# Fetches of row lists declared free of the stores of later groups, in a fused convolution and mixture-of-experts kernel

## The chip, the cores and the metric

The kernel runs on one core of a Trainium2 chip. The metric is the device time of one execution in microseconds (us); less is better. The core has five engines that run side by side, each through its own list of instructions in order: TensorE (PE in the profile, with its weight loads as PEld), VectorE (DVE), ScalarE (ACT), GpSimd (POOL) and SyncE (SP). An instruction that has to wait for a semaphore holds up everything behind it on its engine. Transfers are issued by SyncE and GpSimd and run on 16 shared DMA engines.

## The reference

Inputs: `x` of 8 x 3584 x 192 values, weights for 7 taps of 8 heads per token, and 8 experts of a 192 to 1024 to 192 network. First a causal convolution whose taps are a softmax of each token's own weights, then each token goes to the one expert whose embedding has the largest cosine with it.

```python
w = exp(weight_gen - max(weight_gen)); w = w / (sum(w) + 1e-9)     # over the 7 taps
out[b, s, h] = sum over k of w[b, s, h, k] * x_pad[b, s + k, h]    # causal, 24 values a head
logits = normalized(out) @ normalized(expert_emb).T / tau
expert_idx = argmax(logits); gate_w = softmax(logits)[expert_idx]
result[token] = gate_w * (relu(out[token] @ w1[expert_idx]) @ w2[expert_idx])
```

## The kernel before

The 28672 tokens are worked on in 32 units of 128 x 7 tokens. VectorE multiplies and adds the taps of a unit; for the first five units TensorE does the additions (`sums=5`), in PSUM. ScalarE squares, scales and splits the rows into two 16-bit parts, SyncE turns them with a transposing DMA (`turn`, L519), TensorE computes the logits, VectorE chooses the expert and counts each token's place in its expert's list. GpSimd then writes each token's row into the list of its expert in `lst`, a tensor in device memory, with indirect stores of 128 rows, seven for a unit (`scatter`, L625). A unit's rows stand in one of three buffers, `row_0x` to `row_2x`, in turn.

Units go in 18 groups: the first four of one unit, then 14 of two. After most groups a batch of eight tiles is made, one for each expert, of 256 rows (`T`) or 128 rows (`P`); which, is written in `sizes`. VectorE computes in `schedule` from where in each list the tile is read: only lists with enough rows take part, others read rows that go nowhere. So a tile reads rows that were stored by the time of the batch, while later stores go to places above them in the same list. At the end come 28 tiles of 128 rows for what is left in the lists (`last_batch`), behind `pads` (L1559), which writes empty rows behind each list's end.

A tile begins with `fetch` (L684), called by `load_rows` (L674) on SyncE: it reads the row number into a register, issues a transposing DMA of the rows into `x_0x`, `x_1x` or `x_2x` and a small DMA of the gates and token numbers into one of six `meta` buffers. From the ninth tile on three `x` buffers are used in turn, so a fetch must also wait until TensorE has read the tile three before. For a large tile ScalarE copies a part (`again`), then TensorE does the first layer (`first`, into PSUM banks `bank_..`), ScalarE the relu (`hi`), VectorE the low part (`lo`), TensorE the second layer (into `gram` and `bank_02x`), ScalarE scales it, GpSimd stores it (`out_dram`).

The order on every engine is written out ahead by a planner (`run_steps`): a list of steps with estimated costs and priorities is simulated while the program is built, and each step is issued when its turn comes. `InOrder` (L56) keeps each engine to that order; `behind` (L72) puts instructions that are made elsewhere behind the last one. On SyncE fetches, turns and loads of `x` and of the tap weights stand in one order.

Which instruction waits for which follows from what they read and write. A fetch reads `lst` at a place that is known only when it runs, and a `scatter` writes it at such places, so each fetch depends on every store that was issued ahead of it in the order, also those of later groups. Exceptions are declared: a `scatter` is free of other stores (group `rows`) and of fetches (group `loads`); a fetch joins the group `loads` only. `load_rows` also adds by hand the stores of the groups that are new in its batch, `deps`.

Of the kernel before, what the change touches and what calls it, by code (L numbers as in the profile page):

```python
# [24 lines left out]
    groups=(1, 1, 1, 1, 2, 2, 2, 2, 2, 2, 2, 2, 2, 2, 2, 2, 2, 2),  # L25
# [55 lines left out]
def tile_dynconv_moe(  # L81
# [78 lines left out]
    def raw_ins(i):  # L160
        return getattr(i, "ins", i)
# [51 lines left out]
    rows = [a[:, 0 : U * ROWP].rearrange("p (t r) -> p t r", r=ROWP) for a in packs]  # L213
# [444 lines left out]
    class Tile:  # L658
# [15 lines left out]
        def load_rows(self, row0, deps):  # L674
            def fetch():
                return self.fetch(nc.sync.value_load(row0, min_val=0, max_val=DUMMY))

            for i in SP.behind(fetch):
                i = raw_ins(i)
                tc.add_to_no_dep_group("loads", i)  # L680
                for d in deps:
                    tc.add_manual_dep(i, d.name, sync_dep, reason="rows of the lists")

# [446 lines left out]
    groups, group_of = [], {}  # L1130
# [611 lines left out]
```

## Time and profile before

| what | value |
|---|---|
| median of 3 runs | 1236.18 us (1232.36 to 1238.47) |
| profiled execution | 1239.12 us, of it 1237.3 us from the first to the last instruction |
| mean granted TensorE clock | 0.974 |
| TensorE busy | 1138.2 us (92%), 13376 matmuls |
| TensorE weight loads busy | 997.3 us (81%) |
| VectorE busy | 1018.2 us (82%) |
| ScalarE busy | 802.7 us (65%) |
| GpSimd busy | 616.7 us (50%) |
| DMA moved | 156.15 MB |

Busy time is time in which an engine executes; waiting and issuing of transfers are not in it. SyncE only waits and issues, so it has no busy time, and its timeline shows its transfers. Shares are means over stages that differ: up to about 200 us the first units and the weights are prepared, to about 980 us units and tiles run side by side, then only tiles are left. A wait is put down to what ended it.

### The profile page before, as it was taken

Reading aid. Unit: us, or ns where it says so; the run is one execution under the profiler, and the core shown is the slowest. Engines: PE = TensorE matmul, PEld = TensorE weight load, DVE = VectorE, ACT = ScalarE, POOL = GpSimd, SP = SyncE. Lnnn points to the kernel's source line nnn. Section 1 sums busy time; section 2 is a strip of 40 time slices with the busy share of each in tenths; the row PEclk is TensorE's granted clock in tenths of the full one; section 3 lists DMA queues with packets and bytes.
Section 4 is the critical chain, followed back from the end, with each engine's and each line's share of the span. In section 5 each row is a group of like instructions: output and inputs, shape, how many; then the busy total and the mean of one; then the engine's idle time right before and its main releaser. Section 6 shows DMA issues by size and latency. Waiting matters only on the chain. (4 is left out here: it accounts for less than half of the span.)

```text
span 1237.3 us, 34717 instructions
## 1 busy us (share of the span) xinstructions
PE 1138.2 (92%) x13376; PEld 997.3 (81%) x13376; DVE 1018.2 (82%) x1546; ACT 802.7 (65%) x2036; POOL 616.7 (50%) x566
## 2 busy tenths in 40 slices
PE   5996478989989999989999899999899999999996
PEld 3553267878888898879888788889899989899996
DVE  8997698999988999889899999799797426338884
ACT  1765457779878987979797676566566434444442
POOL 4025143728566584847556576655537352223332
PEclk9998689999999999999999999999999999999999
DMA  9979446566666655755576646554434442112221
GB/s 273 259 188 155 102 124 128 146 139 152 175 138 147 138 141 133 168 129 165 158 140 149 151 126 131 142 103 110 128 61 107 108 118 56 42 44 51 49 43 30
DMA packets 254495, 156.15 MB, mean 126 GB/s; under 512 B 225005, under 2 KB 238565, under 8 KB 251248
## 3 DMA queue, kind: packets, MB, share of 16 engines
q1 hardware_dynamic: 228656, 94.86, 36.3%
q0 software_dynamic: 25664, 58.98, 15.8%
q8 instruction: 106, 1.74, 0.6%
q14 instruction: 69, 0.57, 0.2%
HBM read 62.20 MB, written 46.45 MB: 88 GB/s over the span
## 5 line engine op out<-in xcount | busy, mean ns | idle before, releaser
L66 PEld LDWEIGHTS <-wall 128*128 128x128 f16 (+2 forms) x5316 | 392.7, 99 | 110.7 <-issue 72.7
L66 DVE TENSOR_TENSOR prod_0x<-x_t,w_t 128x1344 f32<-128x1344 f32 x90 | 139.1, 1546 | 0.7 <-PE sums_0x L66 0.7
L66 DVE TENSOR_TENSOR prod_1x<-x_t,w_t 128x1344 f32<-128x1344 f32 x89 | 137.8, 1549 | 0.0
L66 POOL DMA_INDIRECT lst<-row_1x,pos x77 | 101.6, 1320 | 34.3 <-issue 22.2
L66 POOL DMA_INDIRECT lst<-row_0x,pos x77 | 100.7, 1308 | 29.7 <-issue 23.8
L66 POOL DMA_INDIRECT lst<-row_2x,pos x70 | 92.8, 1326 | 41.8 <-issue 21.7
L66 ACT ACTIVATE hi_2x<-bank_00x 128x512 f16<-128x512 f32 x91 | 54.3, 596 | 48.8 <-PE bank_00x L66 28.2
L66 ACT ACTIVATE hi_3x<-bank_10x 128x512 f16<-128x512 f32 x88 | 52.5, 597 | 42.4 <-PE bank_10x L66 22.5
L66 ACT ACTIVATE hi_0x<-bank_01x 128x512 f16<-128x512 f32 x91 | 54.3, 597 | 37.2 <-PE bank_01x L66 25.5
L66 ACT ACTIVATE hi_4x<-bank_11x 128x512 f16<-128x512 f32 x88 | 52.5, 596 | 39.3 <-PE bank_11x L66 24.6
L66 ACT ACTIVATE hi_1x<-bank_12x 128x512 f16<-128x512 f32 x88 | 52.3, 594 | 38.5 <-PE bank_12x L66 26.2
L66 PEld LDWEIGHTS <-hi_1x 128*128 128x128 f16 x744 | 67.6, 99 | 4.6 <-issue 1.8
L66 PEld LDWEIGHTS <-hi_0x 128*128 128x128 f16 x752 | 67.5, 98 | 4.4 <-issue 1.3
L66 PEld LDWEIGHTS <-hi_2x 128*128 128x128 f16 x744 | 66.9, 98 | 3.6 <-issue 0.9
L66 PEld LDWEIGHTS <-hi_3x 128*128 128x128 f16 x704 | 62.8, 98 | 5.4 <-issue 2.6
L66 PEld LDWEIGHTS <-hi_4x 128*128 128x128 f16 x704 | 63.1, 98 | 3.0 <-issue 0.8
L66 DVE TENSOR_TENSOR acc_1x<-acc_1x,prod_1x 128x1344 f32<-128x1344 f32 x42 | 65.0, 1548 | 0.4
L66 DVE TENSOR_TENSOR acc_1x<-acc_1x,prod_0x 128x1344 f32<-128x1344 f32 x42 | 65.0, 1547 | 0.0
L66 PE MATMUL gram<-wall,lo_0x 128*128 128x192 f16 x256 | 63.6, 248 | 0.0
L66 PE MATMUL gram<-wall,lo_1x 128*128 128x192 f16 x256 | 63.0, 246 | 0.0
L66 DVE TENSOR_TENSOR acc_0x<-acc_0x,prod_1x 128x1344 f32<-128x1344 f32 x39 | 60.4, 1549 | 0.3
L66 DVE TENSOR_TENSOR acc_0x<-acc_0x,prod_0x 128x1344 f32<-128x1344 f32 x39 | 60.5, 1550 | 0.0
(434 smaller groups left out, 3614.1 us busy)
## 6 DMA issues: line engine op xcount, KB each, us to landing
x_t<-in_x_dram SPq DMA_DIRECT2D x24, 1248.0 KB
w_t<-in_weight_gen_dram SPq DMA_DIRECT2D x16, 392.0 KB
x_t<-in_x_dram SPq DMA_DIRECT2D x8, 672.0 KB
wall<-in_moe_w_dram POOLq DMA_DIRECT2D x7, 768.0 KB
x_t<-in_x_dram SPq DMA_DIRECT2D x8, 504.0 KB
wall<-in_moe_w_dram POOLq DMA_DIRECT2D x7, 512.0 KB
wall<-in_moe_w_dram POOLq DMA_DIRECT2D x14, 256.0 KB
lst<-pad SPq DMA_DIRECT2D x8, 194.0 KB
```

Of the source, the lines that this page charges most:

```text
L66: self.last = self.tc.keep_in_program_order(op(*args, **kwargs))
```

## The change

One line in `load_rows`. Both transfers of a fetch are declared free of all stores in the group `rows`, with the exception of the stores in `deps`: those of the groups that are new in this batch, and for the last tiles also the pads. Stores of groups that older batches took in had been waited for by the first fetch of those batches, earlier in SyncE's order. The loop at the end for lists that are longer than foreseen calls `fetch` directly and is as before.

```diff
             for i in SP.behind(fetch):
                 i = raw_ins(i)
                 tc.add_to_no_dep_group("loads", i)
+                tc.declare_no_dep(i, group="rows", keep=deps, reason="rows of later groups lie above those that are read")
                 for d in deps:
                     tc.add_manual_dep(i, d.name, sync_dep, reason="rows of the lists")
```

## Rows read from the trace of the kernel before

**Rows 1.** Busy time by stretch: stretch, us, busy us (instructions), clock, DMA share, GB/s.

```profile
200.00:960.00 760.00, 724.33 (x8831) 649.76 (x8829) 686.11 (x909) 579.46 (x1529) 457.33 (x389) 0.99 0.57 136
960.00:1180.00 220.00, 218.65 (x2726) 205.33 (x2724) 122.59 (x249) 96.11 (x212) 73.95 (x70) 1.00 0.28 66
```

**Rows 2.** Waits of SyncE, 200 to 965 us: who, for whom, us, times, longest.

```profile
SPq L66 <- DMA lst<-row_1x,pos: 94.2, 24, 8.9
SPq L66 <- DMA lst<-row_2x,pos: 81.5, 22, 9.5
SPq L66 <- DMA lst<-row_0x,pos: 70.0, 18, 8.8
...
SPq L66 <- DVE row_2x L66: 19.0, 6, 6.0
```

**Rows 3.** Timeline of SyncE: start, us to issue, what it issues.

```profile
471.41 0.42 SPq L66 DMA_DIRECT2D x_t<-in_x_dram  x1
...
583.65 0.36 SPq L66 DMA_DIRECT2D x_t<-in_x_dram  x1
584.83 1.27 SPq L66 DMA_TRANSPOSE x_0x<-lst  x1
...
848.31 1.30 SPq L66 DMA_TRANSPOSE x_0x<-lst  x1
...
871.36 0.36 SPq L66 DMA_DIRECT2D x_t<-in_x_dram  x1
```

**Rows 4.** The chain that ended last: start, us, what; a DMA from issue to landing.

```profile
788.76 4.67 DMA lst<-row_0x,pos
...
872.20 8.41 DMA lst<-row_0x,pos
880.67 2.93 DMA x_0x<-lst
```

**Rows 5.** Timeline of GpSimd: the stores of rows around 757 to 778 us.

```profile
756.01 1.69 POOL L66 DMA_INDIRECT lst<-row_2x,pos  x1 [0.30 <-issue]
...
778.18 1.64 POOL L66 DMA_INDIRECT lst<-row_0x,pos  x1 [1.86 <-issue]
```

**Rows 6.** Timeline of TensorE: matmuls after a gap, in brackets gap and releaser.

```profile
222.94 1.28 PE L66 MATMUL bank_11x<-x_2x,wall 128*128 128x128 f16 x20 [1.80 <-DMA x_2x<-lst]
...
257.59 1.11 PE L66 MATMUL bank_11x<-x_1x,wall 128*128 128x256 f16 x8 [2.68 <-DMA x_1x<-lst]
...
368.44 1.87 PE L66 MATMUL bank_12x<-x_1x,wall 128*128 128x128 f16 x16 [2.98 <-DMA x_1x<-lst]
...
483.04 1.73 PE L66 MATMUL bank_00x<-x_1x,wall 128*128 128x128 f16 x20 [2.76 <-DMA x_1x<-lst]
...
591.47 1.28 PE L66 MATMUL bank_12x<-x_0x,wall 128*128 128x128 f16 x20 [2.86 <-DMA x_0x<-lst]
...
767.09 1.28 PE L66 MATMUL bank_00x<-x_1x,wall 128*128 128x128 f16 x20 [1.71 <-DMA x_1x<-lst]
...
796.61 1.03 PE L66 MATMUL bank_10x<-x_1x,wall 128*128 128x256 f16 x8 [2.20 <-DMA x_1x<-lst]
...
883.65 1.65 PE L66 MATMUL bank_00x<-x_0x,wall 128*128 128x128 f16 x14 [5.43 <-DMA x_0x<-lst]
```

**Rows 7.** Waits of TensorE, 200 to 965 us, of those ended by ScalarE the largest.

```profile
PE bank_00x L66 <- ACT hi_2x L66: 5.0, 2, 3.0
```

**Rows 8.** Waits of ScalarE for fetches, 200 to 965 us.

```profile
ACT x_2x L66 <- DMA x_2x<-lst: 10.1, 5, 3.3
ACT x_1x L66 <- DMA x_1x<-lst: 8.0, 5, 2.7
ACT x_0x L66 <- DMA x_0x<-lst: 5.5, 4, 3.6
```

**Rows 9.** Stretches of low granted clock, first and last of six after 200 us.

```profile
224.28:227.69 3.41, 3.41 (x40) 2.74 (x37) 3.41 (x3) 1.51 (x4) 2.66 (x3) 0.50 0.74 187
...
883.05:886.46 3.41, 2.81 (x25) 2.76 (x25) 0.00 (x0) 0.48 (x1) 0.20 (x1) 0.50 0.32 64
```

## The prediction

> **What bounds the kernel now.** I read the stretches first, then the waits of SyncE, the chain that ended last, TensorE's own timeline and the waits of ScalarE. From 200 to 960 us TensorE is busy for 724.33 of 760.00 us, so 35.7 are lost there; from 960 to 1180 us it is busy for 218.65 of 220.00, which is full [rows 1]. VectorE in the first stretch is busy for 686.11, which leaves it 73.9 us of idle time. So what can be won lies ahead of 960 us, and it reaches the end one for one only where nothing but TensorE sets the pace.
>
> SyncE's queue shows what the edit is about. From 200 to 965 us it sat 64 times (24, 22 and 18), 245.7 us together and 3.8 on average, until an indirect store of rows into the lists (`scatter`) had landed [rows 2]. Some of these waits are needed: the first tile of a batch must wait for the rows of its own groups. But the batch whose first fetch is issued at 848.31 [rows 3] has another one at 880.67, and that one ended a wait for a store issued at 872.20 [rows 4]. A store issued after the first fetch of a batch can't be one that the batch needs, since the first fetch had waited for all of those; it brings rows of the next groups. The other such step of the chain is the store of 788.76, for which the first fetch of a batch waited, at 793.49. This store too is of a later run: the run of stores before it had ended with the one at 756.01, and the next began at 778.18 [rows 5]. The two stores took 4.67 and 8.41 us to land, and the second is followed by 2.93 us for the fetch [rows 4]; from 797 us on the chain is nearly all TensorE.
>
> In TensorE's timeline the reader is to see that its larger gaps end with a fetch: eight of them, 1.80, 2.68, 2.98, 2.76, 2.86, 1.71, 2.20 and 5.43 us, together 22.4 of the 35.7 [rows 6]. Two more, 5.0 us, end with a ScalarE result [rows 7]. ScalarE itself waits 14 times, 23.6 us, for fetches, at the copy that `again` makes of each large tile [rows 8].
>
> **The change, part by part.** It adds no computing instruction and no transfer. For both transfers of each of the 156 fetches it takes away the wait for stores into the lists that are not in `deps`; those in `deps` stay. The order on every engine is written out beforehand by the planner, whose costs the edit doesn't touch, so no instruction moves past another. In a fixed order, a wait taken away can make a later event late only through something shared: the DMA engines or the clock. A few waits that the dropped ones had covered may now be written out (for the store of results that frees a `meta` buffer). I cost them at nothing: they fall into the time in which SyncE idles anyway. Without that cover, at no more than the 0.36 us that the issue of a whole load takes [rows 3], 156 of them would be 56 us of a queue that idled for 245.7.
>
> Now the gaps, one class at a time.
>
> *Fetch held by a store, no load just ahead that is still under way* (gaps at 222.94, 767.09 and 796.61): 1.80 + 1.71 + 2.20 = 5.7 us. The mean hold of 3.8 us is larger than any of the three, so I take all of it; bounds 0 and 5.7.
>
> *Fetch held by a store, with a load of x just ahead of it on SyncE* (483.04 and 883.65). Here one wait hides another. The fetch issued at 584.83, right behind a load of x issued at 583.65, had its matmul begin only at 591.47 [rows 3, 6]: 6.6 us after its issue, against 2.93 on the chain. Counted from the load it is 7.82 us. So the fetch behind the load of 871.36 would be there at 879.2 at the earliest, and if it comes in with the store that travelled beside the same load, at 872.20 + 8.41 = 880.6. TensorE was free at 883.65 - 5.43 = 878.22. The gap shrinks by 3.0 to 4.5 us; I take 3.0, by the store of that very moment. Behind the load of 471.41 the fetch would come at 479.2, before TensorE is free at 480.3, so I take 2.7 of the 2.76. Together 5.7; bounds 0 and 8.2.
>
> The Trainium skill speaks to this: "DMA: Bandwidth & Descriptors", section "Queues, rings and completion order", says that a DMA engine takes the descriptors of one queue in ring order. By it a fetch freed from its semaphore still comes in behind the load, and the 6.6 us above agree; if it did not hold, the gap at 883.65 would close wholly and the sum below be 2.4 us larger.
>
> *Fetch behind a load that itself stands behind a held fetch* (368.44 and 591.47): 2.98 + 2.86 = 5.8 us. These close only as far as the earlier fetch moves up. The mean hold of 3.8 is often enough for that, not always; I take three quarters, 4.4; bounds 0 and 5.8.
>
> *First fetch of a batch, waiting for its own rows* (257.59, 2.68 us): stays. I take nothing.
>
> *Through ScalarE*: 5.0 us [rows 7], the same wait one step on: `again` is late, the relu behind it on ScalarE is late, and TensorE waits for its result. I take three quarters, 3.8; bounds 0 and 5.0.
>
> *The clock.* After 200 us the granted clock fell six times to the lower level (0.50, 1.2 GHz) for 3.41 us; the first and the last are shown [rows 9]. Each begins within 3.5 us after TensorE had fallen idle in one of the gaps above or while it still was. Half of 3.41 is 1.7 us of lost work. I take it away where the gap closes: three of the six (behind 222.94, 483.04 and 796.61), 5.1 us. At 257.59 the gap stays, and at 368.44 and 883.65 a part does. Bounds 0 and 10.2.
>
> What TensorE gets back: 5.7 + 5.7 + 4.4 + 3.8 + 5.1 = 24.7 us.
>
> How much of it reaches the end? After 760 us come the gaps at 767.09, 796.61 and 883.65 and one stretch of low clock: 1.7 + 2.2 + 3.0 + 1.7 = 8.6. From there the chain is TensorE's but for the steps that the edit removes [rows 4], and I carry it whole. The 16.1 us before that lie in shared work: VectorE is busy for 90% of the stretch [rows 1], and ahead of 788 us the chain runs through GpSimd. Carried whole it is 16.1, not at all 0; I take half, 8.0, because TensorE at 95% is the busier of the two, though not by much. Together 16.6 us.
>
> The profiled execution took 1239.12 us: 1239.1 - 16.6 = 1222.5. The median of the runs is 2.9 us below that execution, which gives 1219.6, in round numbers 1220.
>
> **The rivals.** *Another wait takes its place.* SyncE also waits for VectorE before it turns the rows of a unit, 19.0 us in six waits for one of the three row buffers alone [rows 2], and whatever fetch stands behind such a turn stays as late as it was. Against it: just ahead of the fetches for the gaps on the chain stands no such turn. If it holds, only the part after 760 us is left, or less: 0 to 8.6 us, 1228 to 1236. Chance 0.27.
>
> *More than the sum.* The stores of rows stand on GpSimd behind stores of results, which wait for ScalarE, which waits for TensorE, which waits for fetches, which wait for the stores. With that loop cut, the smaller gaps that I didn't count may close as well. The limit is all 35.7 us of TensorE's idle time [rows 1] and 10.2 of low clock: 1236 - 46 = 1190. A likelier point is 30 us, 1206. Chance 0.08.
>
> *Slower.* SyncE comes sooner to the loads of x, which then run ahead of stores of rows; the store beside a load took 8.41 us to land and the other one 4.67 [rows 4], 3.7 more. If that hits the last stores of a group, the first fetch of the batch, which does need them, comes 3.7 us later. Some 15 batches come after 200 us. The 16.6 us and another 6.2 are gone when more than six of them are hit so that TensorE waits; eight cost 30 us, 13 more than the gain: 1249. Against it: of the gaps that I count only the one at 257.59 is of this kind. Chance 0.06.
>
> *No effect.* A wait for a semaphore's count is a wait for all that was counted before; if the stores kept by `deps` share their semaphores with later ones, the fetches could wait as long as now. Against it: the stores in question are issued later than the kept ones, so that their counts are higher. 1236. Chance 0.04.
>
> **How the numbers follow.** The forecast, 10 to 27 us less, has the remaining 0.55; its own range is 1209 to 1226. The limit of 0.5% is 6.2 us, about what a measurement of this kernel can tell from no change. Faster by more: 0.55 + 0.08 and a third of the first rival, 0.72. Within it: the rest of that rival and no effect, 0.22. Slower: 0.06. The range leaves out the deeper half of the second rival, the slower case, and the upper end of the first and the fourth: 1207 to 1235.
>
> **What would show it.** SyncE's waits for stores into the lists should fall from 245.7 to under 90 us. The gaps that now stand at 767.09 and 796.61 should be gone, that at 883.65 should be 2 to 3 us and stand behind a load of x, and the one at 257.59 should stay. ScalarE's 23.6 us for fetches should halve, TensorE's idle time from 200 to 960 us fall to some 15 us, and the low clock to three stretches. The forecast is wrong if these waits go and TensorE's idle time stays, ended by other names: then VectorE or the turns set the pace. It is also wrong if first fetches of batches become late behind loads of x.

## The result and the profile after

The changed kernel takes 1202.53 us (1200.74 to 1206.22, four runs) against 1237.33 for the kernel before in the same comparison: a ratio of 0.9727, 95% interval 0.9688 to 0.9766, 34.8 us less. The direction was forecast, the size was not: 1202.5 lies 17.5 us below the predicted 1220 and 4.5 us below the range.

Busy time by stretch in the profile after (columns as in [rows 1]), with the one stretch of low clock that is left after 200 us:

```profile
200.00:960.00 760.00, 747.63 (x9209) 674.88 (x9209) 698.82 (x945) 592.55 (x1551) 474.68 (x404) 1.00 0.60 141
960.00:1180.00 220.00, 220.00 (x2886) 209.86 (x2884) 138.03 (x267) 96.37 (x213) 71.90 (x65) 1.00 0.23 52
250.60:257.40 6.80, 5.18 (x28) 3.14 (x28) 3.92 (x8) 2.86 (x6) 3.34 (x3) 0.50 0.65 132
```

TensorE's idle time from 200 to 960 us falls from 35.7 to 12.4 us. Of six stretches of low clock, 3.41 us each [rows 9], one of 6.80 is left.

SyncE's waits from 200 to 965 us (who, for whom, us, times, longest):

```profile
SPq L66 <- PE bank_00x L66: 52.4, 21, 8.1
...
SPq L66 <- DVE row_0x L66: 33.5, 7, 7.8
...
SPq L66 <- DMA lst<-row_2x,pos: 9.0, 2, 8.4
SPq L66 <- DMA lst<-row_1x,pos: 7.6, 5, 4.4
SPq L66 <- DMA lst<-row_0x,pos: 6.5, 5, 3.0
```

The 245.7 us that SyncE spent on stores into the lists [rows 2] are 23.1. What it waits for now is room: its waits for TensorE, which must have read an x buffer before it is filled again (the `bank` rows and a few like them), come to 237.3 us where they were 74.9. The fetches now run ahead of TensorE. All waits of TensorE and those of ScalarE for fetches in the same stretch:

```profile
PE bank_11x L66 <- DMA x_1x<-lst: 6.7, 1, 6.7
PE bank_01x L66 <- DMA x_0x<-lst: 2.0, 1, 2.0
PE bank_00x L66 <- ACT hi_2x L66: 1.9, 1, 1.9
PE bank_01x L66 <- ACT lo_1x L66: 0.7, 1, 0.7
PE bank_11x L66 <- DMA x_2x<-lst: 0.6, 1, 0.6
PE bank_01x L66 <- ACT hi_0x L66: 0.5, 1, 0.5
PE bank_11x L66 <- ACT x_2x L66: 0.5, 1, 0.5
```
```profile
ACT x_1x L66 <- DMA x_1x<-lst: 3.0, 1, 3.0
ACT x_0x L66 <- DMA x_0x<-lst: 1.9, 2, 1.3
ACT x_2x L66 <- DMA x_2x<-lst: 0.6, 1, 0.6
```

Seven waits are left where [rows 6] alone show eight large ones, and ScalarE's 23.6 us for fetches [rows 8] are 5.5.

The order of the instructions on TensorE and SyncE is the same before and after, so each matmul and each transfer has its counterpart. The matmuls of 883.65, which waited for 5.43 us, now begin at 845.87 without a gap. Their fetch, issued at 880.67 before, goes out at 836.32, still right behind the load of x that before left at 871.36:

```profile
835.16 0.37 SPq L66 DMA_DIRECT2D x_t<-in_x_dram  x1
836.32 1.58 SPq L66 DMA_TRANSPOSE x_0x<-lst  x1
```
```profile
845.87 1.28 PE L66 MATMUL bank_00x<-x_0x,wall 128*128 128x128 f16 x20
```

The largest gap that remains is at the first fetch of a batch (6.70 us, at 252.22), which needs its own rows; it is longer than its counterpart of 2.68 at 257.59. The last store of those rows left 6.7 us earlier than before (239.80 for 246.46), but took 9.19 us to land, where before the fetch could go out 5.8 us behind it (252.28). The load of x beside it, which left 2.0 us behind that store before (248.42), now left 1.4 us ahead of it:

```profile
238.38 0.53 SPq L66 DMA_DIRECT2D x_t<-in_x_dram  x1
```
```profile
239.80 9.19 DMA lst<-row_2x,pos
249.20 2.97 DMA x_1x<-lst
```

The second gap, 1.97 us at 861.63, stands where before there was none (898.61). SyncE's timeline just ahead of it, and the chain that ended last:

```profile
846.07 1.23 SPq L66 DMA_TRANSPOSE x_2x<-lst  x1
852.79 0.36 SPq L66 DMA_DIRECT2D meta_5x<-lst  x1
853.26 3.41 SPq L66 DMA_TRANSPOSE xT<-row_2x  x1
858.03 2.04 SPq L66 DMA_TRANSPOSE x_0x<-lst  x1
```
```profile
858.03 3.56 DMA x_0x<-lst
861.59 0.04 issue
861.63 1.27 PE bank_01x L66 x20
```

The small transfer into `meta_5x` left 6.7 us after the rows that it belongs to; the longest wait of SyncE between 836 and 862 us is the 5.3 us of the next row, for a store of results out of the same buffer. Behind it comes a turn of a unit's rows (3.41 us to issue), and then the fetch.

```profile
SPq L66 <- DMA out_dram<-o_3x,meta_5x: 5.3, 1, 5.3
```

### The profile page after: what moved, and what is told of

The parts are those of the page before. It is cut to its first block, busy times and chain, and to the rows that moved or that the text cites. A ratio compares the mean times of both kernels' runs of the same rounds, so it can differ in the third digit from the quotient of the medians.

```text
span 1198.8 us, 34709 instructions
## 1 busy us (share of the span) xinstructions
PE 1124.5 (94%) x13376; PEld 990.3 (83%) x13376; DVE 1017.1 (85%) x1546; ACT 803.7 (67%) x2036; POOL 620.2 (52%) x566
## 3 DMA queue, kind: packets, MB, share of 16 engines
q0 software_dynamic: 25664, 58.98, 17.5%
## 4 chain that ended last, share of the span: by engine, by line
PE 78%; DMA 9%; issue 3%; ACT 3%; POOL 3%; DVE 3%; SPq 1%; POOLq 0%; DVEq 0%; ACTq 0%
PE bank_02x L66 18%; PE gram L66 17%; PE bank_12x L66 8%; PE bank_11x L66 8%; PE bank_01x L66 8%; PE bank_00x L66 8%; PE bank_10x L66 8%; DMA wall<-in_moe_w_dram 3%; DMA xT<-row_2x 2%; POOL lst L66 2%; PE g_ps L66 1%; DMA x_0x<-lst 1%; DMA lst<-row_2x,pos 1%; DVE wall L66 1%; SPq L66 1%
## 5 line engine op out<-in xcount | busy, mean ns | idle before, releaser
L66 DVE TENSOR_TENSOR prod_0x<-x_t,w_t 128x1344 f32<-128x1344 f32 x90 | 139.1, 1545 | 0.7 <-PE sums_0x L66 0.7
L66 POOL DMA_INDIRECT lst<-row_0x,pos x77 | 103.3, 1341 | 30.1 <-issue 22.9
L66 POOL DMA_INDIRECT lst<-row_2x,pos x70 | 93.8, 1340 | 43.0 <-issue 22.7
L66 ACT ACTIVATE hi_4x<-bank_11x 128x512 f16<-128x512 f32 x88 | 52.4, 596 | 44.0 <-PE bank_11x L66 26.2
L66 ACT ACTIVATE hi_2x<-bank_00x 128x512 f16<-128x512 f32 x91 | 54.2, 596 | 38.4 <-PE bank_00x L66 20.1
L66 DVE TENSOR_TENSOR acc_1x<-acc_1x,prod_1x 128x1344 f32<-128x1344 f32 x42 | 65.0, 1546 | 0.4
L66 DVE TENSOR_TENSOR acc_1x<-acc_1x,prod_0x 128x1344 f32<-128x1344 f32 x42 | 64.9, 1546 | 0.0
```

The source lines that it names most:

```text
L66: self.last = self.tc.keep_in_program_order(op(*args, **kwargs))
```

## The experiments

The theories: (1) TensorE sets the pace, so that whatever it gets back arrives whole; (2) VectorE and GpSimd share the pace, so that half of what is gained ahead of 760 us is lost on the way, as the prediction had it. Further ones are in the expectations.

The runs were made on two kinds of chips. On one kind the kernel before takes 1236 us, as in the result; on the other three chips 1275 to 1278. Ratios are always against runs of the kernel before on the same chip.

### The parts of the change, on chips with 1275 to 1278 us

A flag on each tile switches the declaration; the variants differ in the condition alone. In it `g` is the group after which a batch is made, and the change of condition at 12 falls near 740 us.

```diff
+                if self.free:
-                tc.declare_no_dep(i, group="rows", keep=deps, ...)
+                    tc.declare_no_dep(i, group="rows", keep=deps, ...)
...
+            t.free = g < 12        # early; late: g >= 12 and the last tiles
+            t.free = size == P     # small, with the last tiles; large: size == TAIL
```

> The declaration stands only for the fetches of the batches up to number 11, whose fetches are issued before some 760 us; the later batches and the last tiles wait for stores as before. Theory 1 (whatever TensorE gets back before 760 us arrives at the end whole): the matmuls of the changed kernel are 26 us ahead at 759 us, 3.3 of which were there before the first fetch, so 20 to 26 us less than the kernel before, about 1213. Theory 2 (the prediction's: half of it is taken up by VectorE and GpSimd on the way): 8 to 13 us less, about 1226. Theory 3 (only the part after 760 us counts): no difference.

> The declaration stands only for the fetches of the batches from number 12 on and of the last tiles, those after some 760 us. Theory 1 (each part brings what TensorE gained in its own stretch): the changed kernel gained 12.4 us between 759 us and the end, so 9 to 14 us less than the kernel before, about 1225; together with the early part the sum is the 34.8 us of the whole change. Theory 2 (the prediction's term for this part): 8.6 us less. Theory 3 (the early part is what keeps the later stretch free of gaps): under 5 us less, and the two parts add up to clearly less than the whole.

> The declaration stands only for the batches of 128-row tiles (seven of them) and the last tiles. Theory 1 (the stores held up these batches most, because their tiles give SyncE and GpSimd the most transfers for the matmuls they feed): the changed kernel gained about 20 us of its 34.8 in these stretches, so 18 to 24 us less than the kernel before, about 1215. Rival (a hold costs the same in either kind of batch, so that the share of fetches decides): half of the gain, some 17 us or less, and no more than the 256-row batches bring alone.

> The declaration stands only for the batches of 256-row tiles. Theory 1: the changed kernel gained about 11 us in these stretches, so 8 to 12 us less than the kernel before, about 1226; with the 128-row batches alone it adds up to the whole 34.8. Rival (a hold costs the same in either kind of batch): 17 us or more less. Theory 2 (a hold removed in one kind of batch is only handed on to the next batch, which still waits): the two parts together fall well short of 34.8.

Measured: early 0.9959 (0.9926 to 0.9991), late 0.9959 (0.9924 to 0.9993), small 0.9893 (0.9831 to 0.9954), large 0.9938 (0.9908 to 0.9968). All four are well below what theory 1 expected. But the kernel before took 41 us more here than in the result, so the yardstick was missing: the whole change on such a chip.

> The changed kernel itself once more, as the yardstick for the parts: the kernel before took 1278 us on the chip of the first four experiments against 1237 where the change was timed, so the size of the gain has to be taken beside its parts on one chip. Theory 1 (every hold of TensorE that goes reaches the end whole): 2.7% less, as in the result, wherever the kernel before takes some 1237 us. Theory 4 (where the kernel before takes some 1278 us, TensorE waits for other things as well, ScalarE's results above all, and the change buys less): 1.0 to 1.8% less there, 13 to 23 us.

> Again the declaration for the batches up to number 11 alone. Theory 1: 1.6 to 2.1% less where the kernel before takes some 1237 us. Theory 2 (half of the gain before 760 us is lost on the way): 0.6 to 1.0% less. Where the kernel before takes some 1278 us: 0.4% less, as in the first run, with the whole at 1.0 to 1.8%.

> Again the declaration for the batches from number 12 on and the last tiles alone. Theory 1: 0.7 to 1.1% less where the kernel before takes some 1237 us, and with the early part it adds up to the whole. Theory 3 (the parts need each other, because a queue that is freed early stays ahead later): under 0.4%, and the sum falls well short of the whole. Where the kernel before takes some 1278 us: 0.4% less, as in the first run.

> Of the two transfers of a fetch only the one that brings the rows is declared; the small one for the gates, which SyncE issues right behind it, still waits for the stores. Theory 1 (SyncE's queue is what is held): the rows of this fetch come at once, but whatever stands behind it in the queue is held as before, so a third to two thirds of the whole gain: 0.9 to 1.8% where the whole is 2.7%. Rival (only the row transfer's own lateness matters to TensorE, the rest of the queue has slack): within 0.3% of the whole.

The last of these declares the transposing transfer only (`if at == 0:` over `for at, i in enumerate(SP.behind(fetch))`). Measured: whole 0.9832 (0.9797 to 0.9866), early 0.9942 (0.9914 to 0.9970), late 0.9977 (0.9945 to 1.0008), rows only 0.9891 (0.9853 to 0.9929). So the change itself brings 1.7% on these chips, the size that theory 4 had. Small and large add up to 1.07 + 0.62 = 1.69%, the whole, but the six runs of small lie between 1254.9 and 1277.9 us (0.995 of the kernel before by their mean), so that this sum is not shown. Early and late do not add up. A third run of them later gave 0.9949 (0.9922 to 0.9977) and 0.9961 (0.9923 to 0.9999), so in the mean of three 0.50% and 0.34%, half of the whole, as theory 3 had it for these chips.

Rows only brings some two thirds (1.09% of 1.68): the small transfer behind it keeps SyncE on stores for 90.8 us from 200 to 965, against 17.0 in the whole change on the same chip. The queue is held by either of the two transfers, and both have to be declared.

What these chips do differently, TensorE's idle time in the whole change that nothing in the profile accounts for, from 200 to 965 us:

```profile
PE bank_01x L66 <- issue: 4.0, 7, 1.3
PE bank_10x L66 <- issue: 2.9, 6, 0.9
PE bank_11x L66 <- issue: 2.9, 5, 1.8
...
```

With the rows left out that is 19.1 us in 45 pieces; all traces from these three chips have 11 to 21 us of it there, and no trace from a chip with 1236 us has any, those of the result among them. VectorE has such pauses too, 5.6 to 12.7 us in the same stretch against 0 to 1.7. TensorE's waits for ScalarE, which theory 4 named as the reason, are 19.2 us in the whole change, against 3.6 in the profile of the result.

### More work on TensorE, on a chip with 1236 us

This asks directly what the prediction answered with "I take half": tiles 24 to 87 repeat the first matmul of their first bank, 4 x 8 x 3 times 256 columns and 4 x 8 x 6 times 128, some 21 us by the traced distance of such matmuls (0.11 and 0.056 us). In the traces the repeats lie between about 330 and 795 us, later than the expectation says.

```diff
                 for i, (wi, b) in enumerate(parts):
+                    if self.n is not None and 24 <= self.n < 88 and q == 0 and i == 0 and g == 0:
+                        for _ in range(3 if self.paired else 6):
+                            PE.matmul(o, lhsT=self.w1(wi, f), rhs=b, start=True, stop=False, ...)
                     PE.matmul(
```

> The kernel before itself, for its trace on the chips of the experiments, on which it takes 1277 to 1278 us against 1237 where the change was timed. Theory 4 (TensorE is stopped there by something that no semaphore shows, beside the holds): its trace has some 20 us of TensorE idle time that the profile lays to nothing ('issue'), as all experiments so far have (19 to 28 us), where the profiles of before and after had 0.0 and 0.2. Rival (the kernel before is slower there because its holds are longer): none of that, and SyncE's waits for stores are well above 245.7 us.

> The kernel before, with matmuls done over again in the first bank of each tile of the eight batches between some 255 and 760 us (the repeats write what the next matmul overwrites): by the traced lengths about 21 us more of TensorE, spread over that stretch. It asks what the prediction answered by half: how much of a time that TensorE loses or gains ahead of 760 us reaches the end. Theory 1 (TensorE sets the pace and everything else follows it): the whole, 18 to 23 us more. Theory 2 (VectorE and GpSimd share the pace): half, 8 to 12 us more. Rival (the holds don't depend on TensorE, so the extra work fits into the gaps that they leave): under 6 us more.

> The changed kernel with the same 21 us of repeated matmuls. Theory 1: the whole arrives here too, so 18 to 23 us more than the changed kernel: about as long as the kernel before where the changed one gains 1.7%, 1.0% faster than it where the changed one gains 2.7%. Theory 2: half, 8 to 12 us more, so still 0.7 to 1.0% faster than the kernel before in the one case and 1.8 to 2.0% in the other.

> The kernel before, without the declaration, but with four buffers for the rows of a tile in place of three once the first ones are free; the order on the engines is planned anew by the same rules. Theory 5 (fetches only come late because they are issued one or two tiles ahead; a fourth buffer gives a held fetch one more tile of time): it brings most of what the declaration brings, 1.2 to 2.5% less. Theory 1 (the hold stands in SyncE's queue itself, whatever number of buffers is free, and a fetch that is issued earlier meets more stores that have not landed): under 0.6% less, or more time than before.

In the trace of before_here TensorE has no idle time that the profile lays to nothing, and SyncE's waits for stores come to 245.8 us from 200 to 965, as in the result. With more work the kernel before takes 1.0082 (1.0047 to 1.0117), 10 us more: half. The changed kernel with the same work takes 0.9899 (0.9852 to 0.9946) of the kernel before, where without it 0.9727 was measured: 1.7% of 1236, 21 us more, with an uncertainty of some 7: whole. Busy time from 260 to 760 us (columns as in [rows 1]) of the kernel before, the same with more work, the changed kernel and the same with more work:

```profile
260.00:760.00 500.00, 481.15 (x5744) 425.02 (x5744) 461.91 (x602) 406.71 (x1074) 310.00 (x261) 1.00 0.61 146
```
```profile
260.00:760.00 500.00, 491.06 (x5895) 436.43 (x5895) 458.17 (x594) 403.48 (x1052) 309.99 (x260) 1.00 0.60 144
```
```profile
260.00:760.00 500.00, 497.33 (x6104) 445.73 (x6102) 481.78 (x636) 417.88 (x1098) 323.19 (x274) 1.00 0.64 151
```
```profile
260.00:760.00 500.00, 498.44 (x6010) 443.99 (x6010) 465.87 (x605) 411.86 (x1078) 313.44 (x266) 1.00 0.62 148
```

In the kernel before TensorE's idle time falls from 18.9 to 8.9 us as work is added (from 34.2 to 22.7 between 200 and 960), while SyncE's waits for stores stay at 241.4 us: about half of the 21 us falls into gaps in which TensorE waited for held fetches anyway. The size is theory 2's, the reason is the rival's. In the changed kernel there are 2.7 us of idle time to fall into. The half is right for the kernel before and wrong for the changed one, since the edit takes away the very gaps that make it a half.

Four x buffers in place of three (`xb=(2, 2)`, order planned anew) leave the kernel before at 0.9976 (0.9945 to 1.0006): its waits for stores are 264.5 us, 19 more than with three. Room does not help a queue that is held for stores, as theory 1 had it.

### VectorE, the parts once more, and a fourth buffer

```diff
-    def taps(u, x_t, w_t, acc):
+    def taps(u, x_t, w_t, acc, n):
+        if 10 <= n < 24:
+            tap(acc, 0, u, x_t, w_t)
         tap(acc, 0, u, x_t, w_t)
```

> The changed kernel with the first multiplication of each of 14 units that VectorE sums (numbers 10 to 23, between some 275 and 630 us) done twice: 14 times 1.47 us, 20.6 us more of VectorE. Theory 1 (TensorE alone sets the pace of the changed kernel): VectorE has some 61 us of idle time in that stretch and a unit is summed well ahead of the batch that needs its rows, so under 6 us more. Theory 2 (VectorE shares the pace, which is why the prediction carried half): 8 to 14 us more. Were VectorE the pace by now: 18 us or more.

> A third time the declaration for the batches up to number 11 alone, for a chip on which the kernel before takes some 1237 us. Theory 1 (in a kernel whose holds ahead of 760 us are gone, what TensorE gains there arrives whole): 1.6 to 2.1% less. Theory 2: 0.6 to 1.0%. Theory 6 (the lead of TensorE meets the holds that are still there after 760 us, as extra work met the gaps of the kernel before): between the two, 1.0 to 1.5%, and the gaps behind 760 us are longer than in the kernel before. On a chip where it takes some 1277 us: 0.4 to 0.6%, as twice before.

> A third time the declaration for the batches from number 12 on and the last tiles alone. Theory 1: 0.7 to 1.1% less where the kernel before takes some 1237 us. Theory 6: with the lead of the early part missing the later stretch has as long holds as in the kernel before, and TensorE gets back what stood there, 1.7 + 2.2 + 3.0 us and a stretch of low clock, 0.5 to 0.8%. On a chip where it takes some 1277 us: 0.2 to 0.4%, as twice before.

> The changed kernel with four buffers for the rows of a tile in place of three once the first ones are free, the order planned anew by the same rules. Theory 1 (nearly all of TensorE's gaps are gone; after 260 us 3.9 us are left in the changed kernel's profile, which stand behind a load and behind ScalarE): within 0.4% of the changed kernel, so 2.3 to 3.1% below the kernel before where that takes some 1237 us. Rival (SyncE now waits for room for x most of the time, 50 to 35 us for each kind of bank, so one more buffer lets it run further ahead): another 0.5% or more.

> The kernel before itself, for one more trace. Theory 4: on a chip where it takes some 1276 us TensorE's idle time that the profile lays to nothing is 17 to 28 us, as in all experiments on such chips, and SyncE's waits for stores are within a tenth of the 265 us of the trace on the faster chip. On a faster chip it is 0.0 us, as there.

> A fourth time the declaration for the batches up to number 11 alone. On a chip where the kernel before takes some 1236 us: theory 1 (whole carry) 1.6 to 2.1% less; theory 2 (half) 0.6 to 1.0%; theory 6 (part of the lead falls into the holds that are left after 760 us, above all the gap that the profile of before has at 883.65) 1.0 to 1.5%. On a slower chip 0.4 to 0.6% less, and against the kernel before on that chip the trace shows the stretch in which the lead ends.

The first four ran on a chip with 1275 us. The first multiplication of each of 14 units done twice on VectorE takes 0.9900 (0.9866 to 0.9934), which against 0.9832 for the change without it on another such chip is 0.7%, some 9 us of 20.6, with an uncertainty of 6. On these chips VectorE's work seems to take a part, against theory 1. How it reaches the end is not shown: TensorE is idle for 28.8 of 500 us between 260 and 760 in the whole change and 27.1 with the additional work, and in neither trace does it wait for VectorE. On a chip of the other kind it was not tried. The fourth buffer on top of the change: 0.9990 (0.9958 to 1.0022), 1.6% slower than the change alone on such chips, which neither theory expected. The order is another one there, and TensorE has no less idle time (29.7 of 500 us); which of its steps costs the time stays open. No version beat the changed kernel.

The last two ran on a chip with 1236 us. So before_again (one execution, 1229.1 us) gave no trace of the slower kind: it has no idle time of TensorE laid to nothing and 237.5 us of waits for stores. (The expectation's 265 us fit the 264.5 of the kernel with the fourth buffer; the kernel before has 245.8.) The declaration for the batches up to group 11 alone, early_4, takes 0.9829 (0.9788 to 0.9871): 21.1 us of 1235.6. The point lies in theory 1's range; the interval, 1.3 to 2.1%, reaches into theory 6's but stays clear of theory 2's, which ends at 1.0%. What the late part adds was not run alone on such a chip; by the difference to the result it is 2.73 - 1.71 = 1.0% or 13 us. In the trace of early_4 the gap that the profile before has at 883.65 (5.43 us, [rows 6]) is still there (4.44 us), since those fetches still wait for stores:

```profile
860.76 2.29 PE L66 MATMUL bank_00x<-x_0x,wall 128*128 128x128 f16 x20 [4.44 <-DMA x_0x<-lst]
```

Ahead of it the same stretch as above reads

```profile
260.00:760.00 500.00, 496.27 (x6045) 442.81 (x6044) 479.24 (x636) 418.50 (x1098) 318.53 (x270) 1.00 0.64 150
```

3.7 us of idle time for the 18.9 of the kernel before. Counted matmul by matmul against before_again on the same chip, early_4 is 12 us ahead at 760 us and 14.5 at the end; against the profile before it is 20 and 24.5. The lead does not shrink on the way.

## Why the prediction was wrong

The mechanism was right, and most of the signs that it named are there: 245.7 us of store waits to under 90 (23.1), the gaps at 767.09 and 796.61 gone, 12.4 us of idle time for "some 15", ScalarE's 23.6 us more than halved; the low clock fell to one stretch for the three foretold. Two signs are not: the gap at 883.65 is gone in place of 2 to 3 us, and the one at 257.59, which should stay, grew. What failed above all is how the gain was carried to the end.

**The step that failed**: "The 16.1 us before that lie in shared work ... I take half, 8.0." The early part alone brings 21.1 us (15.9 to 26.2) where the sum had 8.0. Carried whole, the prediction's own sum is 24.7 us, and 1239.1 - 24.7 - 2.9 = 1211.5, inside its own range; the 9 us from there to the measured time are terms that were short, below. The reason given for the half, VectorE at 90%, does not hold: with the holds gone VectorE is busy for 698.82 us of the stretch, more than before, and TensorE still for 747.63 of 760, at no wait for VectorE. The half of the kernel before is real, but it comes from the gaps: added work falls into them. A gap that is taken away has nothing behind it to fall into.

**The terms of the sum**, from TensorE's waits that are left:

- Held fetches, 11.4 taken of 13.9: only the 0.57 us of 215.97, the counterpart of 222.94, are left, so 13.3. Behind a load behind a held fetch, 4.4 taken: all 5.8 came.
- Through ScalarE, 3.8 taken: 5.0 - 1.94 = 3.1. The 3.0 us at 539.69 are gone; the 2.0 at 703.55 stand at 678.27 with 1.94. There ScalarE had waited for a store of rows (1.2 us) and a fetch (1.0), and now waits for a store of results (3.1).
- First fetch of a batch, 0 taken: minus 4.0, since 2.68 became 6.70. It came at 252.22 for 257.59, but TensorE was ready 9.4 us earlier than before.
- A gap in a new place, not in the sum: minus 2.0 (861.63).
- Small gaps were not in the sum: 35.7 - 22.4 - 5.0 = 8.3 us, of which 12.4 - 6.7 - 2.0 - 1.9 - 0.6 = 1.2 are left: 7.1 more. This is what "more than the sum" had named, at a chance of 0.08; its likelier point, 1206, is the nearest of all to the measured time.
- Clock, 5.1 taken: six stretches of 3.41 to one of 6.80, half of 13.7, 6.8.

Together 30.1 us where the sum had 24.7. The two profiled executions differ by 38.4 us: of the 8.3 that no term covers, 1.4 is TensorE's idle time after 960 us, and some 3 us of lead are there before the first fetch and so do not come from the change. The rest stays open. The terms themselves hold to a few us only, since they come from one execution each: in two other traces of the kernel before the same stretch has 34.2 and 32.6 us of idle time and four stretches of low clock, and its executions on one chip lie between 1228 and 1246 us.

**At the place of 883.65** the forecast of 2 to 3 us, standing behind a load of x, was wrong: the gap is gone, 5.4 us where 3.0 were taken. The prediction moved the fetch up and left the load of 871.36 where it was. But that load itself stood behind a fetch (869.41) that had been held for 8.8 us by a store, and came earlier with it: load and fetch now leave 10.7 and 9.6 us before TensorE reads the rows. The fetch did come in behind the load. The packets of the two transfers in the trace show it: the load's 128 begin between 836.15 and 841.20 us, the fetch's 384 between 840.21 and 842.45, 6.1 us after the fetch was issued. That agrees with the rule that the prediction weighed from the Trainium skill ("DMA: Bandwidth & Descriptors", section "Queues, rings and completion order"), by which the descriptors of one queue are taken in ring order. The order held, and the gap closed all the same, which the prediction had not reckoned with.

**The waits costed at nothing.** Waits of SyncE for stores of results out of `meta` buffers, "written out" once the dropped ones no longer cover them, come to 12.3 us from 200 to 965. One of them stands ahead of the gap at 861.63.

**The rivals.** "Another wait takes its place" came true at two places, 1.97 us at 861.63 and 1.94 at 678.27, not for the kernel. Of "slower" the mechanism is there once: at 252.22 a load of x ran ahead of the last store of a group, the store took 9.19 us to land, and TensorE waited 4.0 us longer; that the load made the store late is likely by this one case, not tested. No other first fetch of a batch leaves a gap of more than 0.6 us.

**Left open**: why three chips show TensorE pauses that no semaphore ends, why the change brings 1.7% there in place of 2.7%, and why early and late do not add up there. No trace of the kernel before from such a chip exists to compare. That VectorE takes no part on the chips with 1236 us is read from TensorE's waits and from early_4; added VectorE work was not run there.

## What to carry to other kernels

A gain is carried to the end by the kernel that is left after the change, not by the one that is profiled: ask whether the gaps that would swallow it are the ones that go, and if they are, carry it whole. Small gaps behind one queue belong into the sum with the large ones: here 7.1 us of 8.3 closed with them. When a held transfer is freed, what stands ahead of it in the queue moves up too, so a load that seems to be in the way need not stay there. When the first fetch of a transfer pair is freed, look at the second one and at what it waits for: declared alone, the rows brought two thirds.

## What was not expected of the hardware

The same kernel takes 1236 us on some chips and 1275 to 1278 on three others, 3% more. VectorE's first product takes 1545 ns in the profile of the result and 1546 in that of the whole change on a slower chip, so single instructions of VectorE are as long there. But TensorE has pauses of up to 2.4 us that the profile lays to nothing, 11 to 21 us together, VectorE has some as well, and TensorE is busy for 1149.5 us with the same 13376 matmuls that take 1124.5 in the profile of the result. The same change is worth 34.8 us on one kind and 21 on the other.
